# Watching the softmax row sums of a fused attention and feed-forward kernel, with a branch to a general path at its end

## The chip, the core and the metric

The kernel runs on one core of a Trainium2 chip. A core has five engines that work side by side, each with its own in-order instruction queue: TensorE (PE; its weight loads are listed apart as PEld), VectorE (DVE), ScalarE (ACT), GpSimd (POOL) and SyncE (SP, which only issues transfers and waits). DMA engines move data between device memory and the on-chip memory, and also bring in instruction code. The metric is the device time of one execution in microseconds (us); less is better.

## What is computed

```python
k_proj = np.einsum('ks,bhsd->bhkd', E, k)
v_proj = np.einsum('ks,bhsd->bhkd', F, v)
scores = (1 / np.sqrt(64)) * np.matmul(q, k_proj.transpose(0, 1, 3, 2))
scores = scores - np.max(scores, axis=-1, keepdims=True)
attn = np.exp(scores)
attn = attn / (np.sum(attn, axis=-1, keepdims=True) + 1e-09)
attn_out = np.matmul(attn, v_proj)            # (8, 8, 1024, 64)
x = attn_out.transpose(0, 2, 1, 3).reshape(8192, 512)
g, val = x @ w_gate, x @ w_val                # (8192, 1536) each
out = (g * (1 / (1 + np.exp(-g))) * val) @ w_out
```

Keys and values of 8 batches and 8 heads are projected from 1024 rows to 64, attention runs over those 64, and a gated feed-forward layer follows. Inputs and output are float32. q, k and v are normal numbers of size 0.1, so that the scores are small; the kernel before uses that the row maximum cancels and leaves it out: exp of a small score can't overflow.

## The kernel before

**Chunks and tiles.** The 8192 tokens are worked in 16 chunks of 512 (two per batch b, ch = 0 and 1; c = 2b + ch). A chunk's feed-forward has 12 tiles f of 128 hidden columns. For each tile, `f_g` (four matmuls into gps, then tanh on ACT into th) and `f_v` (four matmuls into vps, then two DVE steps, s and hT) run; both use L484 for the matmuls. The output product of a chunk is done one chunk later, in 14 pieces `f_m` of six matmuls (L586), with seven products in place of eight: their operands hs are sums of halves of hT, made on POOL (m = 2 and 5, 128x256 each, L569) and on DVE (m = 1, 6, 7). Small adds on ACT, DVE and POOL (L603 to L621) put the pieces together, and SP stores the rows (L622).

**Attention.** A batch has eight units u, each 128 token rows of four heads. `u_S` makes the scores on PE (L353) and their exp on ACT (ee, L357); `u_R` sums each row of 64 and takes the reciprocal on DVE (zz L368, rr L370, 128x8 each); `u_N` multiplies on POOL (L383) into AA or AAd. For batches 1 to 7 two transposing DMAs on SP turn q (qTd, L330) and the normalised rows (AT, L337) into the layout that PE needs; `u_PVt` then makes the chunk's x (pv, L430). `u_KV` and `u_KT` project keys and values of a batch.

**Order.** Everything stands in an order written out by hand. The main loop runs t = 0 to 191, one feed-forward tile each: `f_g`, slot 2t, `f_v`, the pieces of the chunk before (`late`), slot 2t + 1. Attention steps of batch b are put into slots from 48(b-1) on. In the last batch (b = 7, from slot 288) the last unit's `u_S` is in slot 323, its `u_R` and `u_N` in 324; `u_PVt` follows in slots 332 and 344. An opening before the loop loads E, F, the first k, q, v and the weights piece by piece from POOL's queue (L98 to L136), between them the first four units. POOL issues all loads of the loop as well, in line with its arithmetic. After the loop, `f_m_last` finishes the last chunk: DVE steps (L653) and four stores, two from SP and two from ACT (L669). Then the program closes: SP waits for all transfers and engines, and the engines meet at a barrier (L915).

**Buffers.** PSUM has two banks each for gps, vps and a pool "a" (scores, pv and others), and two for yps. `zz` has three buffers, `rr` four.

Of the kernel before, what the change touches and what calls it, by code (L numbers as in the profile page):

```python
# [9 lines left out]
AF = mybir.ActivationFunctionType  # L10
ALU = mybir.AluOpType
AX = mybir.AxisListType
# [3 lines left out]
B = 8  # L16
# [3 lines left out]
KP = 64  # L20
# [7 lines left out]
CH = 2  # L28
# [10 lines left out]
def kernel(  # L39
# [45 lines left out]
    ET = const.tile([P, NJ, KP], BF16, name="ET")  # L85
    FT = const.tile([P, NJ, KP], BF16, name="FT")
# [8 lines left out]
    def load_k(b, h0=0, h1=H):  # L95
        if b:
            kb[b] = kv_pool.tile([P, H, NJ, D], BF16, name="kb", tag="kb")
        nc.gpsimd.dma_start(  # L98
            out=kb[b][:, h0:h1].rearrange("p h j d -> p h (j d)"),
            in_=k[b, h0:h1].rearrange("h (p j) d -> p h (j d)", j=NJ),  # L100
        )
# [36 lines left out]

    kvp = {}
# [115 lines left out]
    def u_KT(b, at="a", prs=(0, NPAIR)):  # L255
# [5 lines left out]
        for pr in range(*prs) if b > 1 else ():  # L261
# [7 lines left out]
        for g in range(2) if b < 2 else ():  # L269
            turn_ksp(t, b, g)  # L270
# [28 lines left out]
    qT, ee, rr, AA, AT = {}, {}, {}, {}, {}  # L299

# [42 lines left out]
    def u_S(b, u, at="a"):  # L343
# [3 lines left out]
        if (b, ch) in BY_DMA:  # L347
# [3 lines left out]
        for n in range(4):  # L351
            slot = (0, 2, 1, 3)[n] if (b, ch) in BY_DMA else n
# [3 lines left out]
        e = aw.tile([P, 4, 2, KP], FP32, name="ee", tag="ee", bufs=4)  # L356
        nc.scalar.activation(  # L357
# [5 lines left out]
        ee[b, u] = e  # L363

    def u_R(b, u):
        e = ee[b, u]
        z = aw.tile([P, 4, 2], FP32, name="zz", tag="zz", bufs=3)
        nc.vector.reduce_sum(out=z[:], in_=e[:], axis=AX.X)  # L368
        r = aw.tile([P, 4, 2], FP32, name="rr", tag="rr", bufs=4)
        nc.vector.reciprocal(out=r[:], in_=z[:])  # L370
        rr[b, u] = r

    def u_N(b, u, eng=nc.gpsimd):
        ch, w = divmod(u, 4)
        g, i = divmod(w, 2)
        if (b, ch) in BY_DMA:
# [3 lines left out]
        else:  # L380
            a = AA[b, u] = first_batch("a", [P, 2, 4, KP], "AA")
            a = a[:]
        eng.tensor_tensor(  # L383
            out=a.rearrange("p j h k -> p h j k"),
            in0=ee.pop((b, u))[:],
            in1=rr.pop((b, u))[:].unsqueeze(3).to_broadcast([P, 4, 2, KP]),
            op=ALU.mult,
        )

# [324 lines left out]

    with tc.manual_schedule():
# [16 lines left out]
        nc.vector.memset(zeros[:], 0.0)  # L732
        make_identity(nc, ident_fp[:])
# [144 lines left out]

        for t in range(NIT):
# [10 lines left out]
        assert not slots and not late  # L890

# [28 lines left out]
```

## Time and profile before

| | us |
|---|---|
| three runs: median (lowest, highest) | 546.88 (546.44, 546.97) |
| the profiled execution: time, and its span from first to last instruction | 546.79, 545.0 |
| granted TensorE clock | 1.000 |
| u_N on POOL, AAd (L383), one of 128x512 | 1.04 |
| hs sum on POOL (L569), one of 128x256 bf16 | 0.69 |
| row sums and reciprocal on DVE (L368, L370), one | 0.68 and 0.20 |
| median from issue to landing: qb, kb, vb loads | 18.4, 10.6, 15.6 |

The span is what the profiler saw between the first and the last instruction; 1.8 us of the time lie around it. The times of one instruction are means over its group. POOL and DVE are busy for about half and three quarters of the span, and wait for others the rest of it. A clock of 1.000 means that TensorE was never throttled.

### The profile page before, as it was taken

To read this page: it belongs to the slowest core of one execution; us is meant where nothing else is said; L and a number is where in the kernel's file an instruction comes from. 1 tells how busy PE (TensorE), PEld (TensorE's weight loads), DVE (VectorE), ACT (ScalarE), POOL (GpSimd) and SP (SyncE) were. 2 spreads that over 40 slices of the span, in tenths; PEclk is the share of its full clock that TensorE was granted. 3 is DMA by queue.
4 is the path that set the end of the run, shared out by engine and by line. 5 is a ranking of instruction groups with operands and counts; after the bars stand their busy time and mean duration, and the time that the engine had idled before them with its cause. 6 is when DMAs were issued, how large, how long until landed. Compare 5 with 4: busy or idle time off the path is not lost.

```text
span 545.0 us, 9374 instructions
## 1 busy us (share of the span) xinstructions
PE 534.2 (98%) x3494; PEld 313.4 (58%) x3556; DVE 412.8 (76%) x697; ACT 232.8 (43%) x416; POOL 294.2 (54%) x364
## 2 busy tenths in 40 slices
PE   8999999999999999999999999999999999999997
PEld 4654445556556555566565665566655665556565
DVE  3787897779668876789777886787967888676884
ACT  3664453354444434444434444434344433443331
POOL 6952393477616854177631865248660655426162
PEclk9999999999999999999999999999999999999999
DMA  9999989929921599008981199512992133110013
GB/s 202 192 196 191 159 155 187 180 75 160 201 68 40 102 186 215 12 30 146 198 160 38 40 144 209 113 40 55 180 206 64 39 78 79 38 40 12 28 40 118
DMA packets 111631, 62.88 MB, mean 115 GB/s; under 512 B 65888, under 2 KB 102752, under 8 KB 111584
## 3 DMA queue, kind: packets, MB, share of 16 engines
q0 software_dynamic: 43952, 29.49, 38.1%
q1 hardware_dynamic: 66800, 31.20, 27.0%
q10 hardware_dynamic: 832, 1.57, 0.9%
q8 instruction: 28, 0.46, 0.3%
q14 instruction: 19, 0.16, 0.1%
HBM read 60.29 MB, written 16.78 MB: 141 GB/s over the span
## 4 chain that ended last, share of the span: by engine, by line
PE 88%; DMA 8%; POOL 2%; issue 1%; ACT 0%; DVE 0%; POOLq 0%; DVEq 0%; ACTq 0%
PE vps L484 28%; PE gps L484 27%; PE yps L586 25%; DMA qTd<-qb 3%; PE sc L353 3%; DMA qb<-in_q_dram 2%; PE kvp L163 2%; DMA Fraw<-in_F_dram 1%; PE pv L430 1%; PE yps L520 1%; DMA wv<-in_moe_w_val_dram 1%; POOL wv L127 0%; POOL AA L383 0%; POOL wg L127 0%; POOL qb L117 0%
## 5 line engine op out<-in xcount | busy, mean ns | idle before, releaser
L496 ACT ACTIVATE th<-gps 128x512 f32<-128x512 f32 x191 | 114.0, 597 | 198.8 <-PE gps L484 178.1
L484 PE MATMUL vps<-xT,wv 128*128 128x512 bf16 (+1 forms) x754 | 195.3, 377 | 0.9
L484 PE MATMUL gps<-xT,wg 128*128 128x512 bf16 (+1 forms) x734 | 192.4, 377 | 1.4
L503 DVE SCALAR_TENSOR_TENSOR s<-th,gps 128x512 f32<-128x512 f32 x191 | 129.2, 677 | 61.5 <-ACT th L496 60.3
L508 DVE SCALAR_TENSOR_TENSOR hT<-s,vps 128x512 bf16<-128x512 f32 x192 | 132.0, 688 | 21.6 <-PE vps L484 1.5
L569 POOL TENSOR_TENSOR hs<-hT 128x256 bf16<-128x256 bf16 x180 | 120.3, 692 | 49.5 <-DVE hT L508 49.5
L484 PEld LDWEIGHTS <-wv 128*128 128x128 bf16 x776 | 73.1, 98 | 85.0 <-issue 6.7
L586 PEld LDWEIGHTS <-hs 128*128 128x128 bf16 x900 | 88.1, 98 | 34.6 <-issue 0.6
L484 PEld LDWEIGHTS <-wg 128*128 128x128 bf16 x776 | 74.0, 98 | 51.7 <-DMA wg<-in_moe_w_gate_dram 0.3
L616 POOL TENSOR_TENSOR tt<-tt,ysb 128x512 f32<-128x512 f32 x28 | 35.6, 1270 | 109.6 <-DVE tt L615 109.6
L383 POOL TENSOR_TENSOR AAd<-ee,rr 128x512 bf16<-128x512 f32 x56 | 58.4, 1044 | 33.6 <-DVE rr L370 32.3
L586 PE MATMUL yps<-ws,hs 128*128 128x256 bf16 x540 | 68.6, 273 | 0.2 <-DVE ysb L653 0.2
L357 ACT ACTIVATE ee<-sc 128x512 f32<-128x512 f32 x64 | 37.9, 595 | 31.9 <-PE sc L353 30.6
L605 POOL TENSOR_TENSOR tt<-xs 128x256 f32<-128x256 f32 x30 | 29.5, 985 | 38.3 <-ACT xs L603 37.7
L586 PE MATMUL yps<-ws,hT 128*128 128x256 bf16 x360 | 48.8, 273 | 0.3
L586 PE MATMUL yps<-wo,hs 128*128 128x256 bf16 x360 | 48.6, 273 | 0.1
L368 DVE TENSOR_REDUCE zz<-ee 128x8 f32<-128x512 f32 x64 | 43.2, 676 | 5.2 <-ACT ee L357 5.1
L569 DVE TENSOR_TENSOR hs<-hT 128x1536 bf16<-128x1536 bf16 (+1 forms) x49 | 45.2, 928 | 0.1
L586 PEld LDWEIGHTS <-hT 128*128 128x128 bf16 x360 | 35.2, 98 | 16.0
L603 ACT COPY xs<-yps 128x512 f32<-128x512 f32 x30 | 17.6, 585 | 28.0 <-PE yps L586 24.7
L610 ACT COPY ysb<-yps 128x512 f32<-128x512 f32 x30 | 17.6, 585 | 27.5 <-PE yps L586 26.6
L439 ACT CAST xT<-pv 128x512 bf16<-128x512 f32 x56 | 28.7, 600 | 0.0
(100 smaller groups left out, 306.0 us busy)
## 6 DMA issues: line engine op xcount, KB each, us to landing
out_dram<-ysb SPq DMA_DIRECT2D x28, 512.0 KB, 2.7
qb<-in_q_dram POOLq DMA_DIRECT2D x14, 512.0 KB, 18.4
kb<-in_k_dram POOLq DMA_DIRECT2D x7, 1024.0 KB, 10.6
vb<-in_v_dram POOLq DMA_DIRECT2D x7, 1024.0 KB, 15.6
wo<-in_moe_w_out_dram POOLq DMA_DIRECT2D x2, 768.0 KB, 21.8
out_dram<-ysb SPq DMA_DIRECT2D x6, 256.0 KB, 2.4
kraw<-in_k_dram ACTq DMA_DIRECT2D x2, 512.0 KB, 4.8
qb<-in_q_dram POOLq DMA_DIRECT2D x4, 256.0 KB, 7.9
```

The costliest lines, as they stand in the source:

```text
L357: nc.scalar.activation(out=e[:].rearrange("p h j k -> p (h j k)"), in_=ps[:].rearrange("p a k -> p (a k)"), func=AF.Exp, scale=scale,)
L368: nc.vector.reduce_sum(out=z[:], in_=e[:], axis=AX.X)
L383: eng.tensor_tensor(out=a.rearrange("p j h k -> p h j k"), in0=ee.pop((b, u))[:], in1=rr.pop((b, u))[:].unsqueeze(3).to_broadcast([P, 4, 2 ...
L439: nc.scalar.copy(out=xT[b, ch][:, kt, :], in_=ps[:])
L484: nc.tensor.matmul(out=ps[:, ts], lhsT=(wg, wv)[w][:, kt, f * P : (f + 1) * P], rhs=x[:, kt, ts], start=(kt == 0), stop=(kt == NKT - 1),)
L496: nc.scalar.activation(out=th[:], in_=ps[:], func=AF.Tanh, scale=0.5)
L503: nc.vector.scalar_tensor_tensor(out=s1[:], in0=th[:], scalar=1.0, in1=g[:], op0=ALU.add, op1=ALU.mult)
L508: nc.vector.scalar_tensor_tensor(out=hT[c][:, f, :], in0=s1[:], scalar=0.5, in1=ps[:], op0=ALU.mult, op1=ALU.mult)
L569: eng.tensor_tensor(out=hs[c, m][:, fs, :], in0=quarter(hT[c], *a)[:, fs], in1=quarter(hT[c], *b)[:, fs], op=op,)
L586: nc.tensor.matmul(out=ps, lhsT=lhsT, rhs=ws[m][:, f, :] if rhs is None else rhs, start=(start and f == 0), stop=(f == HF - 1), skip_group ...
L605: nc.gpsimd.tensor_tensor(out=t[:, 0], in0=xs[:, 0], in1=xs[:, 1], op=ALU.add)
L616: nc.gpsimd.tensor_tensor(out=t[:], in0=t[:], in1=yo[c, p][:, 1:3], op=ALU.subtract)
```

## The change

It adds up the row sums and their reciprocals of all 64 units in a tile `zsum` on POOL, once per `u_N`. Near the end of the last batch's attention a check reduces `zsum` to one number per partition, compares it with 1e25 (not so for infinities or NaNs), counts the good partitions with one matmul, and writes a flag: 0 if all 128 are good, else 1. Every engine loads the flag into a register. At the end of the program each engine branches on it: if it is not 0, a general path computes the whole output again, with each row's maximum taken out before exp; if it is 0, the program closes. With the inputs given here the flag is 0.

Row sums and reciprocals now share one tile `zr` with four buffers. `maxed` is empty while the ordinary path is laid down, and set in `general`, where it selects other branches of the same Python functions.

```diff
+    zsum = const.tile([P, 16], FP32, name="zsum")
+    sane = const.tile([P, 3], FP32, name="sane")
+    flag = const.tile([1, 1], mybir.dt.int32, name="flag")
...
     def u_R(b, u):
         e = ee[b, u]
-        z = aw.tile([P, 4, 2], FP32, name="zz", tag="zz", bufs=3)
-        nc.vector.reduce_sum(out=z[:], in_=e[:], axis=AX.X)
-        r = aw.tile([P, 4, 2], FP32, name="rr", tag="rr", bufs=4)
-        nc.vector.reciprocal(out=r[:], in_=z[:])
-        rr[b, u] = r
+        zr = aw.tile([P, 2, 8], FP32, name="zr", tag="zr", bufs=4)
+        z, r = (zr[:, i].rearrange("p (h j) -> p h j", j=2) for i in range(2))
+        nc.vector.reduce_sum(out=z, in_=e[:], axis=AX.X)
+        nc.vector.reciprocal(out=r, in_=z)
+        rr[b, u] = (zr, r)
...
     def u_N(b, u, eng=nc.gpsimd):
...
+        zr, r = rr.pop((b, u))
         eng.tensor_tensor(
             out=a.rearrange("p j h k -> p h j k"),
             in0=ee.pop((b, u))[:],
-            in1=rr.pop((b, u))[:].unsqueeze(3).to_broadcast([P, 4, 2, KP]),
+            in1=r.unsqueeze(3).to_broadcast([P, 4, 2, KP]),
             op=ALU.mult,
         )
+        nc.gpsimd.tensor_tensor(out=zsum[:], in0=zsum[:], in1=zr[:].rearrange("p i n -> p (i n)"), op=ALU.add)
...
+    def u_sum():
+        nc.vector.reduce_sum(out=sane[:, 0:1], in_=zsum[:], axis=AX.X)
+        nc.vector.tensor_single_scalar(out=sane[:, 1:2], in_=sane[:, 0:1], scalar=1e25, op=ALU.is_le)
+
+    def u_flag():
+        ps = bank("a", [P, 1], FP32, "bad")
+        nc.tensor.matmul(out=ps[0:1], lhsT=sane[:, 1:2], rhs=sane[:, 2:3], start=True, stop=True)
+        nc.vector.tensor_single_scalar(out=flag[:], in_=ps[0:1], scalar=P - 0.5, op=ALU.is_le)
+
+    def u_bad():
+        bad.append(nc.values_load(flag[:], min_val=0, max_val=1, skip_runtime_bounds_check_because="is_le gives 0 or 1"))
+
+    def general():
+
+        for d in (kb, vb, qb, xT, hT, kvp, qT, ee, rr, AA, AT, hs, xx, zz, tt, yo):
+            d.clear()
+        maxed.append(True)
+        ring["wide"] = False
+        by_dma.extend((0, ch) for ch in range(CH))
+        for b in range(B):
+            load_k(b)
+            load_v(b)
+            u_KV(b)
+            u_KT(b)
+            for ch in range(CH):
+                c = CH * b + ch
+                load_q(b, ch)
+                u_TD(b, ch)
+                for u in range(4 * ch, 4 * ch + 4):
+                    u_S(b, u)
+                    u_R(b, u)
+                    u_N(b, u)
+                u_AD(b, ch)
+                u_PVt(b, ch, (0, 1), ("aa", "yz"))
+                for f in range(NFT):
+                    f_g(c, f)
+                    f_v(c, f)
...
         nc.vector.memset(zeros[:], 0.0)
+        nc.vector.memset(zsum[:], 0.0)
+        nc.vector.memset(sane[:], 1.0)
...
+        for s, fn in ((38, u_sum), (40, u_flag), (46, u_bad)):
+            put(48 * (B - 2) + s, fn)
         for t in range(NIT):
...
         f_m_last(NC - 1)
         assert not slots and not late
+
+    with tc.If(bad[0] != 0):
+        with tc.manual_schedule():
+            general()
```

In slots: `u_sum` is in 326, `u_flag` in 328, `u_bad` in 334. In the built program the five engines' streams up to the branch differ from before by these instructions alone: 64 adds on POOL, two memsets, a reduction and two compares on DVE, one matmul on PE, and a register load on each engine. Behind the branch lie first the general path, then a short block for the flag 0 (each engine raises its semaphore to the value that it would have after the general path; SP does so for eight transfer queues, one after the other), then the closing waits, of which SP now has twelve instead of nine. Instructions of the general path: PE 6,873, ACT 1,158, DVE 1,125, POOL 354, SP 129.

More of the change, by code (lines that the diff above doesn't have):

```diff
@@ L95, in load_k @@
     def load_k(b, h0=0, h1=H):
-        if b:
+        if b or maxed:
             kb[b] = kv_pool.tile([P, H, NJ, D], BF16, name="kb", tag="kb")
@@ L136, in load_wo @@
         )
+    maxed = []
     kvp = {}
@@ L260, in u_KT @@
         t = bank(at, [P, NPAIR, KP], FP32, "kTp")
-        for pr in range(*prs) if b > 1 else ():
+        for pr in range(*prs) if b > 1 or maxed else ():
             nc.tensor.matmul(
@@ L268, in u_KT @@
             )
-        for g in range(2) if b < 2 else ():
+        for g in range(2) if b < 2 and not maxed else ():
             turn_ksp(t, b, g)
@@ L299 @@
     qT, ee, rr, AA, AT = {}, {}, {}, {}, {}
+    by_dma = list(BY_DMA)
     kept = {"q": (0, (5, 2)), "a": (0, (1, 6, 7))}
@@ L346, in u_S @@
         ps = bank(at, [P, 4, P], FP32, "sc")
-        if (b, ch) in BY_DMA:
+        if (b, ch) in by_dma:
             t = qT[b, ch, "d"][:].rearrange("p (h i) t -> p i h t", i=2)[:, i, 4 * g : 4 * g + 4]
@@ L351, in u_S @@
         for n in range(4):
-            slot = (0, 2, 1, 3)[n] if (b, ch) in BY_DMA else n
+            slot = (0, 2, 1, 3)[n] if (b, ch) in by_dma else n
             nc.tensor.matmul(
@@ L356, in u_S @@
         e = aw.tile([P, 4, 2, KP], FP32, name="ee", tag="ee", bufs=4)
+        ee[b, u] = e
+        if maxed:
+            exp_maxed(e, ps)
+            return
         nc.scalar.activation(
@@ L362, in u_S, with exp_maxed @@
         )
-        ee[b, u] = e
+    def exp_maxed(e, ps):
+        m = aw.tile([P, 2, 8], FP32, name="m", tag="zr", bufs=4)
+        s = ps[:].rearrange("p h (j k) -> p (h j) k", j=2)
+        nc.vector.reduce_max(out=m[:, 0], in_=s, axis=AX.X)
+        nc.vector.tensor_scalar_mul(out=m[:, 1], in0=m[:, 0], scalar1=-scale)
+        for i in range(8):
+            nc.scalar.activation(
+                out=e[:, i // 2, i % 2, :], in_=s[:, i], func=AF.Exp, bias=m[:, 1, i : i + 1], scale=scale
+            )
     def u_R(b, u):
         e = ee[b, u]
-        z = aw.tile([P, 4, 2], FP32, name="zz", tag="zz", bufs=3)
-        nc.vector.reduce_sum(out=z[:], in_=e[:], axis=AX.X)
-        r = aw.tile([P, 4, 2], FP32, name="rr", tag="rr", bufs=4)
-        nc.vector.reciprocal(out=r[:], in_=z[:])
-        rr[b, u] = r
+        zr = aw.tile([P, 2, 8], FP32, name="zr", tag="zr", bufs=4)
[3 more added lines that the diff above has]
+        rr[b, u] = (zr, r)
     def u_N(b, u, eng=nc.gpsimd):
@@ L375, in u_N @@
         g, i = divmod(w, 2)
-        if (b, ch) in BY_DMA:
+        if (b, ch) in by_dma:
             if (b, ch, "d") not in AA:
@@ L713, in run_slot @@
             fn(*a)
+    bad = []
+    def u_sum():
[31 more added lines that the diff above has]
+                    f_v(c, f)
+                for m in (1, 2, 5, 6, 7):
+                    h_sum(c, m, 0, HF, nc.vector)
+                for n in range(14):
+                    f_m(c, n)
     with tc.manual_schedule():
```

## The prediction

> **What bounds the kernel now.** I read the page first: busy shares, then the groups, to see which engine has no room.
>
> ```profile
> PE 534.2 (98%) x3494; PEld 313.4 (58%) x3556; DVE 412.8 (76%) x697; ACT 232.8 (43%) x416; POOL 294.2 (54%) x364
> ...
> PE 88%; DMA 8%; POOL 2%; issue 1%; ACT 0%; DVE 0%; POOLq 0%; DVEq 0%; ACTq 0%
> ```
>
> TensorE (PE) is busy 534.2 of 545.0 us and has 88% of the chain that ended last. Anything on PE's own queue costs its own time; work on DVE, ACT or POOL costs nothing until it makes PE wait. The stages show where the remaining idle time lies.
>
> ```profile
> 0.00:60.00 60.00, 56.37 (x393) 30.91 (x398) 41.23 (x80) 30.46 (x61) 32.42 (x46) 1.00 1.32 195
> 60.00:450.00 390.00, 387.33 (x2522) 226.74 (x2572) 304.82 (x512) 169.72 (x300) 220.37 (x267) 1.00 0.69 119
> 450.00:530.00 80.00, 79.53 (x488) 46.77 (x496) 59.48 (x91) 29.69 (x53) 36.19 (x46) 1.00 0.13 40
> 530.00:545.00 15.00, 10.96 (x94) 8.98 (x92) 7.23 (x15) 2.93 (x5) 5.19 (x7) 1.00 0.29 107
> ```
>
> Columns: stage, PE, PE loads, DVE, ACT, POOL busy, clock, DMA. From 60 to 530 us PE is idle 3.1 us of 470. The last 15 us have 4.0 us of idle PE, nearly all of it after its last matmul. So there are three places to price: the opening (PE's waits below), the full middle, and the end.
>
> ```profile
> PE warm L754 <- DVE zeros L732: 1.2, 1, 1.2
> PE sc L353 <- DVE BD L151: 0.7, 1, 0.7
> PE sc L353 <- DMA qTd<-qb: 0.4, 1, 0.4
> ```
>
> The list of PE's waits has no POOL in it at all; the 0.4 us at 59.9 us is the end of a chain of loads that POOL issues. For the end, the records of the output tile and of SyncE (SP):
>
> ```profile
> L669 ACTq DMA_DIRECT2D out_dram<-ysb x2: 363/363/363, 540.1 to 541.7; - x2
> ...
> DMA to landing us min/median/max: 2.0/2.5/3.1
> ...
> SPq L915 <- DMA out_dram<-ysb: 2.3, 3, 1.1
> ```
>
> The last matmul ends at 541.2, the last DVE step at 541.65, ACT's last store is issued 541.68 to 542.04 and lands at 543.82. SP then steps through its closing waits (records 61 ns apart, done at 544.19), and drains and barrier take to 545.03: 1.2 us from landing to end, of which 0.83 after SP's drain. The profiled execution took 546.79 us, 0.09 below the median of 546.88; I add to 546.79.
>
> **The adds (64 on POOL).** Each unit's u_N gets a 128x16 f32 add. No row has that size. POOL's L605 add of 128x256 f32 takes 0.73 us where undisturbed and L616 of 128x512 1.27, so 2.1 ns an element and 0.19 us fixed: 0.22 us. Bounds: 0.10 (POOL's 128x1 memset) and 0.69 (the 128x256 bf16 add, L569). I take 0.22, on the line through the two nearest forms of the same operation. In all 64 x 0.22 = 14 us of POOL, which has 251 us idle. Queued behind an add are the next normalisation, the hs sums, the load issues, and through them the AT transposes on SP. The tightest I find: AT issued at 185.0, landing up to 18.9 us later (203.9), read by pv at 206.3. Cover 2.4 us against 4 x 0.22 = 0.9 in that chunk: price 0 in the middle. Without that cover it would be up to 0.9 a batch, 6 us in all.
>
> In the opening there is less cover. Four adds (three behind normalisations from 13.2 to 18.6 us, one between weight loads) come before the loads that the chain follows to the 59.9 us wait: 0.9 us of later issues. Traffic stands at 195 GB/s over these 60 us, so most of a later issue is absorbed by transfers already queued. Bounds: -0.4 (the wait disappears) and +2.8 (four at 0.69, all passed on); I take +0.2, near the bandwidth-bound case. The two small memsets on DVE lie before a 2.8 us wait for kraw: 0. Sums and reciprocals go to one tile zr instead of two: same operations, still four buffers, now released by the add, under 0.3 us later and four units ahead of reuse: 0.
>
> **The check (slots 326 and 328).** A reduction, two compares on DVE of about 0.20 us each (the 128x8 reciprocal, L370, takes 0.203): 0.6 us, covered by DVE's idle 0.9 us before s in most tiles. The reduction waits for the last add; the last normalisation ends at 458.45, the add about 458.7, and DVE is busy with hT until 458.97: no wait. Then one f32 matmul on PE with one column. The f32 turn of E (L742) does 8 in 1.06 us: 0.13 each. Bounds 0.13 and 0.47 (load and matmul records, 0.20 + 0.27, in series). I take 0.13.
>
> **The register load (slot 334, each engine).** PE's stands between a weight load and its matmul; everything of PE is queued behind it. No row shows such a load. Bounds for its length: 0.05 (PE's event-semaphore records, 51 ns) and 2.14 (the last store's issue to landing, a full trip through memory). But PE's sequencer runs ahead: its semaphore wait before L353 was handled at 104.26, the matmul ran at 105.79, and PE had no gap over 0.05 us there. So 1.5 us is covered, and the price is 0 to 0.64, without that lead up to 2.14. I take 0.1, from the lower half. DVE, ACT, POOL and SP load too; ACT idles 1.78 us before most tanh, and DVE's delay would have to pass two gps banks: 0. [...]
>
> **The branch at the end.** All five streams now jump over the general path: 6,873 instructions on PE, 1,158 on ACT, 1,125 on DVE, 354 on POOL, 129 on SP. Two costs.
> First, more closing steps on SP after the store lands. Before: five waits left, then the drain. After, in the not-taken block: five semaphore steps left after the third store (0.30 us), a branch (about 0.10), then twelve waits (0.73) and the drain (0.07), then 0.83: 543.82 + 2.03 = 545.85, that is +0.82, if every jump is free.
> Second, the jump itself. Instruction code arrives by DMA:
>
> ```profile
> q8 instruction: 28, 0.46, 0.3%
> q14 instruction: 19, 0.16, 0.1%
> ```
>
> Queue 8 fits PE (28 packets of 16 KB are 7,168 instructions of 64 bytes, PE has 7,108); queue 14, with 8 KB packets, then serves the others, 0.1% x 16 x 545 / 19 = 0.46 us each. A target that isn't there must be fetched. Bounds: 0.47 (the packet alone) and 5.2 us (Eraw's read, issue to landing). I take 2.5 (the output's median trip in the quiet end) plus 0.5 = 3.0. SP's stream reaches the branch at 541.4: 544.5; eight steps 0.49, branch 0.1, twelve waits 0.73, drain 0.07, barrier 0.83: 546.7, +1.7. ACT, from 542.05, comes to 545.2 and its semaphore is among SP's last waits: no later. At 5.2 us: +3.9. If SP's short jump finds its code present, ACT decides: 545.25 + 0.9 = 546.15, +1.1.
> [...]
>
> **Sum.** 0.2 + 0.13 + 0.1 + 1.7 = +2.1: 548.9 us.
>
> **The rivals.**
> - The jump hides behind the store's landing (547.7). One mechanism: fetches shorter than 543.82 - 541.4 = 2.4 us on SP and 2.8 us on ACT leave only SP's extra steps, 546.79 + 0.82 + 0.13. For: the packets take under 0.5 us. Against: a trip needs a request and a landing, 2.0 us at the least in any store here. This is not slower, by under 0.2% (1.1 us, about what a measurement of this kernel can tell from no change).
> - PE's register load is not covered. Then up to 2.14 more on PE: 551.0. For: it sits between a weight load and its matmul, and its result has a semaphore of its own. Against: the lead of 1.5 us.
> - The adds break POOL's cover. At 0.69 us four make 2.8, 0.4 over the 2.4 us of cover, in some six batches 2.4, and the opening up to 2.6 more: about 552. Against: PE never waits for POOL now.
> - Faster: later loads at the start leave the transposes alone. All idle of PE before 530 us is 6.8 us; it would have to win 3.2 us to come out 0.2% ahead, at a place where 0.4 is on view.
> - The flag comes out set and the general path runs: over 1,070 us (as many matmuls once more). The sum of positive numbers far below 1e25 is compared, so hardly.
>
> **How the numbers follow.** Forecast 0.58 (its own range 548.1 to 550.8: fetch between 2.4 us and 5), hidden jump 0.16, PE's load 0.13, POOL 0.08, faster 0.02, general path 0.03. Slower 0.58 + 0.13 + 0.08 + 0.03 = 0.82, same 0.16, faster 0.02. The range takes in the hidden jump below and PE's load above: 547.6 to 551.3.
>
> **What would show it.** The span grows by about 2 us; PE's busy time and its 60 to 450 us stage stay within 0.3 us; the last store is issued within 0.6 us of 541.7, and from there to the end it is 5 us instead of 3.35. Wrong: a PE gap near 470 us, PE waits for AT or hs, POOL adds over 0.5 us, or an end that is under 1 us longer.

## The result, and the profile after

| | before | after |
|---|---|---|
| median (lowest, highest), us | 546.92 (546.44, 548.63), 6 runs | 551.56 (550.69, 552.51), 6 runs |
| ratio after / before, 95% interval | | 1.0083 [1.0065, 1.0100] |
| profiled execution: time, span | 546.79, 545.0 | 552.51, 550.6 |
| granted TensorE clock | 1.000 | 0.993 |

The change costs 4.6 us; 2.0 were forecast. The page of the changed kernel, shares and chain:

```profile
PE 535.0 (97%) x3496; PEld 313.7 (57%) x3558; DVE 413.3 (75%) x702; ACT 233.0 (42%) x416; POOL 306.0 (56%) x428
...
q8 instruction: 30, 0.49, 0.4%
q14 instruction: 26, 0.21, 0.1%
...
PE 88%; DMA 8%; ACT 1%; issue 1%; POOL 1%; DVE 1%; DVEq 0%; ACTq 0%
```

PE still sets the time. Its busy time rose by 0.8 us and POOL's by 12, and there are nine more packets of instruction code. The stages (columns: stage, its length, PE, PE loads, DVE, ACT, POOL busy, clock, DMA) show where the 5.6 us of this execution went:

```profile
0.00:60.00 60.00, 55.15 (x385) 30.57 (x390) 40.01 (x80) 30.14 (x60) 34.22 (x54) 0.97 1.27 186
60.00:450.00 390.00, 386.54 (x2517) 225.88 (x2563) 303.63 (x510) 168.61 (x298) 229.10 (x318) 1.00 0.69 120
450.00:530.00 80.00, 79.47 (x486) 46.38 (x495) 60.09 (x95) 30.79 (x54) 35.92 (x49) 1.00 0.14 40
530.00:545.00 15.00, 13.88 (x114) 10.86 (x111) 9.60 (x20) 3.41 (x6) 6.80 (x9) 1.00 0.20 77
545.00:550.60 5.60, 0.00 (x0) 0.00 (x0) 0.00 (x0) 0.00 (x0) 0.00 (x0) 0.65 0.28 95
```

In the first 60 us PE does 1.2 us less work than before, at a clock of 0.97 instead of 1.00. The 0.8 us that PE is less busy from 60 to 450 us is its wait for qTd, which now ends at 62.6 us, inside this stage (at 59.9 before); the rest of the middle is as dense as before. The last 5.6 us hold no computing at all. The finest measure is the step hT, which each of the 192 tiles has once on DVE: its start in this execution against its start before.

| later than before by, us | tile 24 | tile 96 | tile 164 | tile 166 | tile 190 | last DVE step | end of the span |
|---|---|---|---|---|---|---|---|
| after | 2.69 | 2.69 | 2.69 | 2.91 | 2.91 | 2.92 | 5.54 |

Three jumps and nothing else: 2.69 in the opening, 0.22 at the matmul of the check, 2.62 between the last DVE step and the end. From tile 24 to 164 the adds cost nothing, and the register load (between tiles 166 and 168) cost PE nothing. The waits of PE in the opening:

```profile
PE efp L809 <- DMA Eraw<-in_E_dram: 1.5, 1, 1.5
PE warm L821 <- DVE zeros L797: 1.2, 1, 1.2
PE sc L358 <- DMA qTd<-qb: 0.8, 1, 0.8
PE sc L358 <- DVE BD L155: 0.7, 1, 0.7
PE vps L505 <- DMA wv<-in_moe_w_val_dram: 0.3, 1, 0.3
```

Of these, Eraw and wv are new and qTd has doubled. And the end: the last four stores before (line 669), then those after (line 690) and what SP waited for:

```profile
DMA to landing us min/median/max: 2.0/2.1/2.5
```

```profile
L690 SPq DMA_DIRECT2D out_dram<-ysb x2: 344/344/344, 542.6 to 543.9; - x2
L690 ACTq DMA_DIRECT2D out_dram<-ysb x2: 362/366/369, 543.0 to 544.6; - x2
...
DMA to landing us min/median/max: 2.2/4.1/4.4
```

```profile
SPq L961 <- SPq L961: 4.1, 3, 2.9
```

The stores take 4.1 us to land (median) where they took 2.1, and SP stands for 4.1 us at three of its steps behind the branch. How the landings and the steps hang together is taken up with the experiments on the end.

### The profile page after: what moved, and what is told of

The parts are those of the page before. It is cut to its first block, busy times and chain, and to the rows that moved or that the text cites. A ratio compares the mean times of both kernels' runs of the same rounds, so it can differ in the third digit from the quotient of the medians.

```text
span 550.6 us, 9480 instructions
## 1 busy us (share of the span) xinstructions
PE 535.0 (97%) x3496; PEld 313.7 (57%) x3558; DVE 413.3 (75%) x702; ACT 233.0 (42%) x416; POOL 306.0 (56%) x428
## 4 chain that ended last, share of the span: by engine, by line
PE 88%; DMA 8%; ACT 1%; issue 1%; POOL 1%; DVE 1%; DVEq 0%; ACTq 0%
PE vps L505 27%; PE gps L505 27%; PE yps L607 25%; DMA qTd<-qb 3%; PE sc L358 3%; PE kvp L167 3%; DMA qb<-in_q_dram 2%; PE pv L451 1%; PE yps L541 1%; DMA wv<-in_moe_w_val_dram 1%; DMA Eraw<-in_E_dram 1%; POOL wv L130 0%; PE warm L821 0%; ACT ee L366 0%; PE efp L809 0%
## 5 line engine op out<-in xcount | busy, mean ns | idle before, releaser
L403 POOL TENSOR_TENSOR AAd<-ee,zr 128x512 bf16<-128x512 f32 x56 | 58.4, 1044 | 30.9 <-DVE zr L389 30.0
L626 POOL TENSOR_TENSOR tt<-xs 128x256 f32<-128x256 f32 x30 | 28.1, 936 | 36.7 <-ACT xs L624 36.1
L388 DVE TENSOR_REDUCE zr<-ee 128x8 f32<-128x512 f32 x64 | 43.3, 677 | 6.1 <-ACT ee L366 6.0
```

The lines of the kernel that those rows point to most:

```text
L388: nc.vector.reduce_sum(out=z, in_=e[:], axis=AX.X)
L403: eng.tensor_tensor(out=a.rearrange("p j h k -> p h j k"), in0=ee.pop((b, u))[:], in1=r.unsqueeze(3).to_broadcast([P, 4, 2, KP]), op=ALU.mult,
L626: nc.gpsimd.tensor_tensor(out=t[:, 0], in0=xs[:, 0], in1=xs[:, 1], op=ALU.add)
```

## The experiments

Times are medians (lowest to highest). "End" is the time from the end of the last DVE step to the end of the span, 3.38 us before. End, hT and Eraw (its time from issue to landing) are read from one profiled execution of each kernel. The kernels of one group were measured beside the kernel before on the same chip; its medians were 546.70, 546.59, 546.59, 546.69 and 546.76 in the five groups.

### The parts of the change, one at a time

**The adds alone.** No check, register load, branch and general path.

```diff
-        for s, fn in ((38, u_sum), (40, u_flag), (46, u_bad)):
-            put(48 * (B - 2) + s, fn)
...
-    with tc.If(bad[0] != 0):
-        with tc.manual_schedule():
-            general()
```

> The ordinary path with the 64 adds, the shared tile zr and the two memsets; no check, no register load, no branch. Theory A (the opening is later because the first four adds push back the weight and q loads issued on POOL): about 548.1 us, 1.0 to 1.5 over before, all of it gained in the first 60 us of the span, and PE's waits for qTd or weights grow by as much. Rival B (the later opening in the profile of the changed kernel came from the TensorE clock falling to half for 3.4 us, by chance of when its window falls): within 0.4 us of before, and the 60 to 450 us stage the same in both.

Measured: 547.66 (546.97 to 548.62), ratio 1.0019 [1.0010, 1.0028]; end 3.30. The profiled execution took 546.97, the lowest time, and there hT is 0.13 late from tile 24 to the end: nothing in the middle. The 0.96 between the medians is nearest to Theory A, but this execution does not show where it arises; the runs on the opening below do.

**Adds, check and register loads, no branch.**

```diff
-    with tc.If(bad[0] != 0):
-        with tc.manual_schedule():
-            general()
```

> The adds, the check and the register loads, without the branch and without the general path. Theory A (the parts add up, and the short jump of the run with four instructions behind its branch cost nothing): adds run + 0.23 (matmul) + 0.35 (register load on PE) = 547.66 + 0.58 = 548.2, within 0.4 of that run's 547.86; end 3.3 us; markers of hT shift by +0.2 to +0.25 at the matmul (tile 165) and by +0.3 to +0.4 around the load (tile 168). Rival B (matmul and load are covered, and the branch cost the short-jump run its +1.2): within 0.3 of the adds run, 547.4 to 547.9, no shift of the markers. Rival C (the load costs its full trip on PE): over 549.

Measured: 548.09 (547.39 to 548.35), ratio 1.0024 [1.0014, 1.0034]; end 3.33. hT is 1.04 late from tile 24 to 164, 1.26 from 166 to the last step. So the matmul costs 0.22, as in the changed kernel, and the load 0. The 0.35 that the expectation gave to the load came from the last tile (191) read alone; tile 190 before it and the last DVE step behind it show no such shift. Theory A's sum held, with one of its terms wrong; the markers show 0.22 of the 0.5 by which this run's distance to the kernel before exceeds that of the adds alone.

**A branch over four instructions.** Everything but the general path.

```diff
-            general()
+            ysb = yo[NC - 1, 0]
+            nc.vector.tensor_copy(out=ysb[:, 0], in_=ysb[:, 1])
+            nc.scalar.copy(out=ysb[:, 2], in_=ysb[:, 0])
+            nc.gpsimd.tensor_tensor(out=ysb[:, 3], in0=ysb[:, 2], in1=ysb[:, 0], op=ALU.add)
+            nc.sync.dma_start(out=rows_of(NC - 1)[:, 0, 0:HC], in_=ysb[:, 3])
```

> Everything of the change, but the branch's body is one small instruction on each of DVE, ACT, POOL and SP in place of the general path, so that the jump is short (and SP has one semaphore step in the block for flag 0, not eight). Theory A: the end costs 0.4 us over before (SP's longer closing list alone), no engine pauses after its branch, total about 549.1. Rival C (SP's steps): only seven steps of 0.07 us are gone, about 551.0.

Measured: 547.86 (547.80 to 549.27), ratio 1.0024 [1.0013, 1.0035]; end 3.33. A branch over little code costs nothing at the end, not even the 0.4 of Theory A; Rival C falls. Its block for the flag 0 has one semaphore step on SP instead of eight, so that this run says nothing on those eight; a later one does. From here to the changed kernel's 551.56 it is 3.70 us (3.3 to its repeat, 551.14), all from the presence of the general path.

**The branch alone.** No adds, sum and matmul in the ordinary path; the flag is set to 0 at the start, loaded in slot 334, and the branch stands over the whole general path.

```diff
-        nc.gpsimd.tensor_tensor(out=zsum[:], in0=zsum[:], in1=zr[:].rearrange("p i n -> p (i n)"), op=ALU.add)
+        if maxed:
+            nc.gpsimd.tensor_tensor(out=zsum[:], in0=zsum[:], in1=zr[:].rearrange("p i n -> p (i n)"), op=ALU.add)
...
+        nc.vector.memset(flag[:], 0)
...
-        for s, fn in ((38, u_sum), (40, u_flag), (46, u_bad)):
+        for s, fn in ((46, u_bad),):
```

> No adds and no check on the ordinary path; the flag is set to 0 by a memset at the start, each engine loads it in slot 334 and branches at the end over the whole general path. Theory A: the load costs PE 0.35 and the end 2.6 us (code of the jump's target is fetched only when the branch runs), so 549.9 us; the last DVE step to the end of the span takes 6.0 us as in the changed kernel, against 3.4 before. Rival C (the end is longer by SP's additional semaphore steps, the fetch is hidden behind the store's landing): +0.8 at the end, about 548.1 in all.

Measured: 550.47 (549.56 to 552.49), ratio 1.0076 [1.0063, 1.0089]; end 5.66. The branch over the general path alone costs 3.8 us, of which the end shows 2.3, near Theory A; the load's 0.35 in it is not there (hT is 0.29 late from tile 24 to 190).

### The adds in the opening

**Without the first four adds, general path in place.** The row sums of units 0 to 3 of batch 0 are not watched.

```diff
-        nc.gpsimd.tensor_tensor(out=zsum[:], in0=zsum[:], in1=zr[:].rearrange("p i n -> p (i n)"), op=ALU.add)
+        if b or u > 3 or maxed:
+            nc.gpsimd.tensor_tensor(out=zsum[:], in0=zsum[:], in1=zr[:].rearrange("p i n -> p (i n)"), op=ALU.add)
```

> The changed kernel without the adds of the four units in the opening (their row sums are left out of the check). Theory A: about 1.2 us faster than the changed kernel, 550.3, with the opening as before. Rival B: as the changed kernel, 551.5, because the adds had nothing to do with the opening.

Measured: 550.52 (550.17 to 552.27), 1.04 below the changed kernel; end 5.75. The medians speak for the adds, but the profiled execution still had a bad opening, hT 2.56 late. So there are two causes in the opening. The next runs take them apart, first with the branch over four instructions.

**Without the first four adds, short branch.** The same edit on the run with the short branch.

> The run with the short jump (general path left out, four small instructions behind the branch) without the adds of units 0 to 3 of batch 0, whose row sums are not watched. Theory A (those four adds, between the load issues on POOL, cost 0.4 to 1.0 us in the opening): 0.4 to 1.0 us below that run's 547.86, so 546.9 to 547.5 at a time before of 546.6 to 546.7, and the waits for wv and qTd before 62 us are as in the kernel before. Theory B (the four adds cost nothing, the differences of the opening are chance or come from the general path): within 0.3 of 547.86.

Measured: 546.69 (546.45 to 547.01), ratio 1.0001 [0.9992, 1.0010]. Four adds of 64 made 1.17 us of difference, a little more than Theory A's 0.4 to 1.0, and without them the kernel is as fast as before.

**All 64 adds, the first four behind the last load issue, short branch.**

```diff
+        if b or u > 3 or maxed:
+            u_Z(zr)
+        else:
+            held.append(zr)
+
+    held = []
+
+    def u_Z(zr):
         nc.gpsimd.tensor_tensor(out=zsum[:], in0=zsum[:], in1=zr[:].rearrange("p i n -> p (i n)"), op=ALU.add)
...
         load_wo(1)
+        for zr in held:
+            u_Z(zr)
```

> The run with the short jump (general path left out) with all 64 adds, but the adds of units 0 to 3 stand on POOL behind the last weight load (wo) instead of between the load issues. Theory A (what costs is that these adds make the loads behind them late): as the run without them, 546.5 to 547.1, no wait for wv at 21 us and none over 0.4 for qTd at 60 us. Theory B (the adds cost wherever they are, or the buffers held longer make DVE wait): 547.5 to 548.2.

Measured: 546.89 (546.74 to 547.50), ratio 1.0005 [0.9996, 1.0014]. The adds' number costs nothing; their place did. The line of the transposes of q shows the chain, in the run with the short branch and the adds at their first place:

```profile
L335 SPq DMA_TRANSPOSE qTd<-qb x14: 1565/3412/7067, 42.1 to 408.2; - x14
```

and with the four moved:

```profile
L335 SPq DMA_TRANSPOSE qTd<-qb x14: 1568/3534/7170, 40.8 to 405.6; - x14
```

The first transpose starts at 42.1 and 40.8 us (41.15 before). In the trace, the four adds take 0.22, 0.21, 0.66 and 0.25 us on POOL, between 14.2 and 22 us; POOL issues the last three q loads of the opening at 24.84, 25.57 and 30.36 us, and at 23.77, 24.50 and 29.64 with the adds moved (before: 23.73, 24.46, 29.53). The last of them lands at 42.04 instead of 40.80: 0.7 us of later issue became 1.2 of later landing. PE's waits follow, first with the adds in their place, then with them moved:

```profile
PE sc L358 <- DMA qTd<-qb: 0.9, 1, 0.9
PE vps L505 <- DMA wv<-in_moe_w_val_dram: 0.8, 1, 0.8
```

```profile
PE vps L513 <- DMA wv<-in_moe_w_val_dram: 0.9, 1, 0.9
```

The wait for qTd is gone. That for wv at 21 us is not: it comes and goes between kernels (0.3 in the changed one, 0.7 in that with the branch alone, which has no adds), so Theory A had one of its two waits wrong.

**The same order with the general path.** The edit of the last diff, on the changed kernel.

> Whole change, with the adds of units 0 to 3 on POOL behind the last weight load. Theory A: 1.0 to 1.2 us under the changed kernel, 550.2 to 550.7, with the end of 5.7 to 6.0 us unchanged; what then remains over the short-jump run with the same order is the end's 2.6 and whatever the general path's code costs the opening (0 if there is no such cost, 1.0 to 1.4 by the runs so far). Theory B (adds' place is nothing): 551.3 to 552.

Measured: 550.36 (549.58 to 552.09), ratio 1.0068 [1.0056, 1.0080]; end 5.58. This is 1.2 below the changed kernel (0.8 below its repeat in the same group), as Theory A says, and 3.47 above the run with the short branch and the same order: the end has 2.26 more, and some 1.2 remain for the opening.

**The first four adds on DVE, with a prefetch hint.** Directly behind their reciprocals; the hint is that of the next part.

```diff
+        if not b and u < 4 and not maxed:
+            nc.vector.tensor_tensor(out=zsum[:], in0=zsum[:], in1=zr[:].rearrange("p i n -> p (i n)"), op=ALU.add)
```

> As the run with the hint, and the adds of the first four units are done on DVE directly behind their reciprocals, instead of on POOL between the opening's load issues. Theory A (those four POOL adds make later loads late and cost 0.4 to 1.0 us in the opening): 0.4 to 1.0 us below the run with the hint, about 547.3 to 547.9. Rival B (the opening's differences come from when the first loads land and when TensorE's clock steps, by chance): within 0.3 us of the run with the hint, and the waits for Eraw, wv and qTd before 62 us differ no more than they do between runs of the kernel before.

Measured: 551.86 (551.22 to 552.90), 1.0 above the run with the hint alone. Neither theory holds. In its profiled execution PE's clock came up at 10.64 us instead of 6.5, which hides what the adds do; four runs don't settle whether that is their doing.

### The end

**A prefetch hint for the branch.** Although its call is written behind the loop, the hint runs at the start of each engine's stream (0.70 to 0.82 us); the short block lies behind the general path, as in the changed kernel.

```diff
+        tc.mark_branch_hint_location("close", "LikelyTaken", engines=[nc.tensor.engine, nc.vector.engine, nc.scalar.engine, nc.gpsimd.engine, nc.sync.engine])
         f_m_last(NC - 1)
...
-    with tc.If(bad[0] != 0):
+    with tc.If(bad[0] == 0, preferred_fallthrough_block=False, label="close") as arm:
+        pass
+    with arm.Else():
```

> Whole change, but each engine is told at the start of the program, by a branch prefetch hint, that the branch at the end will be taken and where it goes; the general path stays between the branch and its target. Theory A (the end's extra time is the fetch of code that lies behind 6,873 instructions, and the fetch can be made early): the end, from the last DVE step to the end of the span, falls from 6.0 us to 3.3 to 3.9; the last stores land 2.0 to 2.3 us after issue (median) instead of 3.9, because no code packets stand before a sixteenth of theirs; the time is 546.7 + 0.58 (matmul and register load of the check) + 0.4 to 1.4 (opening) = 547.7 to 548.7. Rival B (the hint is lost over 545 us, or the fetch still starts at the branch): end 5.6 to 6.0, time 550.3 to 551.6. Rival C (the far jump is slow for another reason than its fetch, such as a flush of five engines' streams): code packets move to before 541 us, but the end stays above 5 us.

Measured: 550.82 (550.71 to 551.87), ratio 1.0083 [1.0070, 1.0097]; end 6.01. The records of the branches, from the trace (us from the end of the branch's record to the engine's first instruction behind it; for PE the length of its branch record; the last row is the run with the branch over four instructions):

```
                     PE     DVE    ACT    SP
after               4.16   3.54   3.74   2.87
hint                0.48   0.53   1.65   3.06
four instructions   0.23   0.38   0.13   0.14
```

The hint works: PE and DVE no longer stand at the branch, ACT half as long. The end doesn't move, so what PE, DVE and ACT lose at the branch is not what sets it here. Theory A's mechanism is half right, Rival B's numbers are right for another reason. The stores show which:

```profile
L690 SPq DMA_DIRECT2D out_dram<-ysb x2: 344/344/345, 541.0 to 542.3; - x2
L690 ACTq DMA_DIRECT2D out_dram<-ysb x2: 362/368/373, 541.4 to 542.9; - x2
...
DMA to landing us min/median/max: 2.1/3.9/4.4
```

They still land late. The packets in the trace say why. In the changed kernel the third store has 144 packets: 135 run from 544.81 to 545.80, on time, and nine, a sixteenth, from 546.78 to 547.91. Between 544.83 and 547.49 run five packets of code, one of 16 KB and four of 8 KB, nearly one after the other. With the hint it is the same picture, with code between 543.37 and 546.21. In the changed kernel the landings reach SP at 547.25, 548.33 and 548.49, and SP's first steps behind the branch start at 547.27, 548.35 and 548.51: each starts when a store has landed. In the run with four instructions one 8 KB packet comes, after the last store's are through.

ACT's own wait is close behind the stores, though. In the changed kernel ACT is back from its jump at 549.09, and SP asks for ACT's semaphore at 549.61, 0.51 us later; in its repeat and the three other runs of the same layout (the branch alone, without the first four adds, and with these moved) it is 0.13 to 0.38. By this reckoning stores on time alone would have shortened the end by that and no more. In the run with the hint ACT is 2.9 us ahead, and the stores alone hold the end.

**The short block in front of the general path.** The engines run on into it and jump behind it.

```diff
-    with tc.If(bad[0] != 0):
+    with tc.If(bad[0] != 0, preferred_fallthrough_block=False):
```

> Whole change, laid out the other way: the short block for the flag 0 stands directly behind the branch, the general path behind that, so that an engine runs on into the short block and then jumps over the general path to the closing waits. Theory A (any jump over the general path waits for a fetch of code at the end): the short block's steps no longer wait, the jump behind them does; the end is 5.3 to 6.3 us, the time 550.5 to 551.8, and stores still land late by some 1.5 us. Rival B (it is only the place of the short block that costs): end 3.3 to 4.0, time 547.8 to 549.

Measured: 553.27 (552.30 to 554.41), ratio 1.0130 [1.0114, 1.0145]; end 6.81. Theory A's direction, worse than its numbers: PE (4.42), DVE (4.02) and ACT (4.31) wait at the second jump, the stores land up to 4.2 us after issue, and SP goes through the last six of its eight steps behind the last landing before it can jump as well.

**Transfers alone behind the branch.**

```diff
             load_k(b)
             load_v(b)
-            u_KV(b)
-            u_KT(b)
             for ch in range(CH):
-                c = CH * b + ch
                 load_q(b, ch)
                 u_TD(b, ch)
...
+                AA[b, ch, "d"] = aw.tile([P, 4, H, KP], BF16, name="AAd", tag="AAd")
+                nc.vector.memset(AA[b, ch, "d"][:], 0.0)
                 u_AD(b, ch)
...
+                    nc.sync.dma_start(
+                        out=rows_of(CH * b + ch)[:, p::2, :], in_=ysb[:].rearrange("p (j x) d -> p j (x d)", j=2)
+                    )
```

> Whole change, but the general path holds its transfers alone (loads, transposes, stores of all eight batches, 97 instructions on SP and 51 on POOL, one on PE and ACT); its arithmetic is left out. The block for the flag 0 has SP's eight semaphore steps again. Theory A (in the opening the descriptors of the many transfers make the first loads late; at the end SP's eight steps behind the last landing cost 0.8 us by themselves): Eraw takes 5.5 us or more from issue to landing instead of 5.0 to 5.2, the end is 3.3 + 0.8 = 4.1 us with stores landing 2.0 to 2.2 us after issue, time 549.2 to 549.8. Theory B (both come from the size of the code): Eraw 5.0 to 5.2, end as in the run with the short jump, 3.3 to 3.5, time 547.6 to 548.3.

Measured: 549.78 (549.39 to 550.54), ratio 1.0056 [1.0042, 1.0069]; end 5.22; Eraw 5.2. The last landing is at 546.69 and the span ends 2.07 later, where the run with one SP step has 1.26. So SP's eight steps, with the closing waits that they push behind the last landing, cost 0.81, as Theory A and the prediction had it. The last store also landed 3.1 us after issue: its last nine packets start at 545.44, when the first of two 8 KB packets of code (from 545.13 and 545.32) ends. So the end is 1.1 above Theory A's. Eraw was on time, against Theory A: the transfers behind the branch don't delay the opening.

**Code on PE alone**, on the run with the short branch.

```diff
+            t = bank("v", [P, CW], FP32, "far")
+            for _ in range(3436):
+                nc.tensor.matmul(out=t[:, 0:P], lhsT=ident_bf[:], rhs=ident_bf[:], start=True, stop=True)
```

> The run with the short jump, with 3,436 small matmuls (6,873 instructions) added behind PE's branch, so that PE alone has as much code to jump over as in the changed kernel; the general path's other work is left out, and SP has one semaphore step. Theory A (PE's amount of code makes the first loads late in the opening, and PE's fetches hold a part of the last stores): Eraw takes 5.5 us or more, PE's branch takes about 4 us, the last store lands 3 us or more after issue, the end is 4.3 to 5.2 us, time 549.3 to 550.5. Theory B (PE's fetch is over before the last store lands, and the first loads depend on something else): Eraw 5.0 to 5.2, end 3.3 to 3.6 us, time 547.6 to 548.4.

Measured: 551.25 (550.51 to 552.14), ratio 1.0088 [1.0074, 1.0102]; end 4.80; Eraw 5.5. The mechanism is Theory A's: PE's branch takes 3.78, and the stores wait. One 16 KB packet of code runs from 544.23 to 545.28; only then do the held packets of the second store start, and those of the third (546.23 to 546.88) and fourth (546.88 to 547.53) queue behind them:

```profile
L690 ACTq DMA_DIRECT2D out_dram<-ysb x2: 362/366/370, 542.9 to 544.4; - x2
...
DMA to landing us min/median/max: 2.1/3.5/3.8
```

The last landing, at 547.94, is 1.26 before the end. The time is above the expected range since the opening was late as well.

**One batch behind the branch.**

```diff
-        for b in range(B):
+        for b in range(1):
             load_k(b)
             load_v(b)
             u_KV(b)
```

> Whole change, but the general path redoes batch 0 alone (860 instructions on PE, 143 each on ACT and DVE, 46 on POOL, 17 on SP); the other seven batches are left out of it. Theory A (the cost goes with the code jumped over on each engine): SP and POOL jump short, ACT and DVE and PE still fetch, fewer code packets stand before the last stores; the end is 0.8 (SP's eight steps) above 3.3 and up to 1 us more, 4.1 to 5.2 us; Eraw 5.0 to 5.2; time 548.5 to 549.9. Theory B (any taken jump beyond the next packet costs the same): end 5.6 to 6.0 us, time 550.3 to 551.6.

Measured: 550.95 (550.11 to 551.74), ratio 1.0081 [1.0067, 1.0095]; end 5.83; Eraw 5.4. Theory B: a general path of an eighth of the code costs as much at the end. PE's branch over 860 instructions takes 3.98, ACT's over 143 takes 2.77; DVE's over 143 takes 0.52 only. So on PE the distance makes little difference here (4.16 over 6,873 in the changed kernel); why DVE's branch over as many instructions as ACT's takes so much less is not shown.

**Hint and moved adds together.**

> As the run before this one, with the branch prefetch hint on every engine. Theory A (the hint saves the engines' own stall, but code packets still hold a sixteenth of the last stores, and SP's eight steps stay): 0 to 0.8 us under the run before this one, 549.4 to 550.7; end 5.2 to 6.0. Theory B (the hint's better run was chance): same as the run before this one within 0.3.

Measured: 551.01 (549.51 to 552.44), ratio 1.0069 [1.0056, 1.0082]; end 6.32, stores landing up to 4.5 us after issue. Neither theory holds: the hint gains nothing over the moved adds alone (550.36), and the median is 0.65 above them.

### The opening with the general path

**The changed kernel once more**, unaltered.

> The changed kernel unaltered, for a second look at its opening beside the others of this call. Theory A (the general path's code makes Eraw land late): Eraw 5.4 us or more from issue to landing again, wv and qTd waits as in the short-jump run; 551.0 to 552.0. Theory B (the first look was chance): Eraw 5.0 to 5.2, time about 550.5.

Measured: 551.14 (550.48 to 552.78), ratio 1.0084 [1.0071, 1.0097]; Eraw 5.9, end 5.58. Theory A, with hT 2.64 late after the opening.

**Code on DVE, and code on PE**, each on the run with the short branch and the moved adds: 6,872 memsets behind DVE's branch, or the 3,436 matmuls of above behind PE's.

```diff
+            for _ in range(6872):
+                nc.vector.memset(zsum[:], 0.0)
```

> The run with the short jump and the moved adds, with 6,872 small memsets on DVE added behind DVE's branch; the general path's work is left out. Theory A (any engine's amount of code makes Eraw land late): Eraw 5.4 us or more, opening 0.4 to 2.6 us later, DVE's branch takes 2 to 3.8 us; end 3.3 to 4.8 us as code packets hold stores; time 547.9 to 550.5. Theory B (PE's code alone does it): Eraw 5.0 to 5.2, opening as in the run without the memsets, end 3.3 to 4.8; time 546.9 to 548.5.

> The same with 3,436 small matmuls (6,873 instructions) on PE instead of the memsets. Both theories: Eraw 5.4 us or more, an opening 0.4 to 2.6 us later, end 4.5 to 5.0 us as in the earlier run with code on PE alone (4.80); time 548.6 to 550.8. If Eraw lands within 5.2 us, the link between code and opening falls.

Measured, on DVE: 548.09 (547.44 to 548.66), ratio 1.0027 [1.0016, 1.0037]; end 4.22, hT 0.55 early after the opening. On PE: 549.74 (548.94 to 551.27), ratio 1.0054 [1.0042, 1.0067]; end 4.95, hT 2.17 late. The transfers' view (size, median us from issue to landing), DVE first, then PE:

```profile
kraw<-in_k_dram ACTq DMA_DIRECT2D x2, 512.0 KB, 4.7
Eraw<-in_E_dram SPq DMA_DIRECT2D x1, 256.0 KB, 5.2
```

```profile
kraw<-in_k_dram ACTq DMA_DIRECT2D x2, 512.0 KB, 5.2
Eraw<-in_E_dram SPq DMA_DIRECT2D x1, 256.0 KB, 5.7
```

Theory B: it is PE's code. Over all kernels, one profiled execution each: the eight with no or next to no code behind PE's branch have Eraw at 5.0 to 5.2 us, the twelve with 860 instructions or more have it at 5.4 to 6.9. The rows don't say how PE's code does this: kraw's first packets start at 1.9 us in all, and are then slower. That part stays open.

What 0.5 us of Eraw then costs is chance in part, and goes by PE's clock. In the changed kernel, stretches of the opening:

```profile
3.93:7.34 3.41, 1.92 (x12) 1.10 (x11) 0.85 (x2) 0.12 (x1) 3.41 (x6) 1.00 1.22 263
7.34:10.76 3.42, 3.42 (x14) 1.68 (x14) 1.33 (x3) 0.94 (x3) 1.92 (x3) 0.50 1.39 200
10.76:14.17 3.41, 2.48 (x26) 1.68 (x25) 0.93 (x4) 1.88 (x5) 0.74 (x1) 1.00 1.42 200
```

PE's clock had come up at 3.93 us, its 11 warming matmuls ended at 5.1, and PE waited 1.5 us for Eraw. In the next 3.42 us it was busy all the time at half the clock; at the full clock that work would take 1.7 us less (an estimate, half of the 3.42). In the kernel before the clock came up at 6.47 us and stayed up. (The 1.000 given for it counts from there: the warming matmuls ahead of 6.47 us end 0.43 us apart, those behind it 0.21, so PE was not at its full clock from the start.)

Two such first stretches at the full clock, from the run with code on PE alone, where the clock then fell, and from that with the short branch and without the first four adds, where it stayed up:

```profile
4.34:7.75 3.41, 2.28 (x15) 1.40 (x13) 1.28 (x4) 0.63 (x2) 3.41 (x5) 1.00 1.34 249
3.93:7.34 3.41, 2.38 (x15) 1.44 (x13) 1.48 (x3) 0.53 (x2) 3.41 (x6) 1.00 1.30 245
```

This fall of the clock parts the openings of all kernels. In the seven profiled executions that have it, hT at tile 24 is 2.17 to 2.69 late; in the others it lies between 0.55 early and 1.68 late (2.12 in the run with adds on DVE, whose clock came up at 10.64 us). With the first four adds at their place and no fall, runs with code behind PE's branch (1.03, 1.11, 1.68) are as late as those without (0.13, 1.04, 1.10, 1.66). All seven have that code. So what it costs the opening is, by these rows, the fall of the clock; it fell where PE waited 1.1 us or more for Eraw in that stretch, and this wait hangs on the landing of Eraw and on the moment at which the clock came up; no run sets the two apart. The other executions agree in the main: with the general path and the moved adds, the times are 549.58 at a granted clock of 0.999, 549.85 and 550.18 at 0.997, 550.54 at 0.996, 551.99 and 552.09 at 0.995. The changed kernel's six are less orderly (551.26 at 0.999).

## Why the prediction came out as it did

"Slower" was right; the size was not. By medians, in the order in which the parts were put in: all adds with the first four moved, the check, the loads and a short branch +0.2 (546.89 against 546.69); the four adds at their place +1.0 (547.86); the general path +3.7 (551.56), of which 2.2 to 2.7 are the end's and the rest the opening's.

- **Adds in the middle, 0:** right. An add takes 0.22 us (median), as worked out from the two larger forms, and hT doesn't shift from tile 24 to 164. The rival of a broken POOL cover falls for the middle.
- **Adds in the opening, +0.2:** mis-sized; +1.0 to +1.2 by the pairs with the short branch and 0.6 to 1.2 by those with the general path. The chain was the right one (four adds, 0.9 us of later issues: 0.7 to 1.1 measured; one add took 0.66). The step that failed is "most of a later issue is absorbed by transfers already queued": nothing was absorbed, for 0.7 us of later issue of q's last load made its landing, and the first transpose behind it, 1.2 us later than with the adds moved, and PE's wait for it, on view before with 0.4, took that over. The bounds (to +2.8) held it.
- **Check matmul on PE, +0.13:** 0.22, within its bounds. The term counted one step of 0.13; the trace shows this f32 matmul as two records of 0.164, each with a weight load.
- **Register load on PE, +0.1:** 0. The load's record is 0.485 us on PE's queue, under the 1.5 us of lead; the five engines' records are 0.47 to 0.55. The rival that it stays uncovered falls.
- **SP's extra steps, +0.82:** right: 2.07 us from the last landing to the end instead of 1.22; the run with transfers alone shows the same 2.07 without any far jump on PE, DVE and ACT. The 0.10 for a branch in the sum is shown by no run: in the changed kernel SP's first closing wait follows its last step by 0.07 (548.86 to 548.93), and from the last landing (548.49) to that wait it takes 0.44 where the sum has 0.30 + 0.10.
- **The jump, 3.0 us:** too small for the wait (3.5 to 4.2 on PE, DVE and ACT in the changed kernel), though inside its bounds; that the wait is one for code fits the packets of code that run meanwhile (one of 16 KB from 544.83 to 545.78, in PE's 543.01 to 547.17). What failed is the step from it to the end. The sum let SP come late to a store that had landed at its usual time, 2.1 us after issue. In fact, while packets of code run, a sixteenth of the third store waits (nine of its packets, until 546.78), and the last store lands 3.9 us after issue. That is 1.8 us, and with the steps 2.6 instead of 1.7 (2.2 in the repeat). The run with the hint shows it: 0.48 and 0.53 us at the branch on PE and DVE, and the same end. That ACT is "no later" held by 0.51 us only (0.17 in the repeat), since its wait took 3.74. The rival of a hidden jump counted on the same undisturbed landing.
- **Missing altogether:** the general path's code on PE makes the first loads land later (Eraw 5.4 us or more instead of 5.0 to 5.2), and in the seven executions in which PE then waited 1.1 us or more for Eraw its clock fell to half. The sum has no term for either. No view before the change shows the late loads; between pairs of runs that differ in PE's code alone (1.2 and 1.9) or in the whole general path (1.0 and 1.2), 1.0 to 1.9 us are left when the end's share is taken off.
- **Faster, and the general path running:** neither happened.
- **The signs named beforehand:** no PE gap near 470 us, as forecast. PE's busy time and its stage from 60 to 450 us moved by 0.8 where 0.3 was allowed; the stage's 0.8 is the wait for qTd, and hT shows no shift from tile 24 to 164. Four of the 64 adds took 0.66 to 0.96 us, over the 0.5 that was to be a sign against the forecast; the three of them in the middle cost nothing. The last store is issued 2.9 us later instead of within 0.6, which is the opening, and from there to the end it is 6.0 us instead of 5.

The range's upper end, 551.3, was 0.3 below the median. It was built from one rival at a time; the terms that went wrong (adds in the opening, the end, and the opening's cost of code that had no term) add up. That the range came so near owes something to the price of a register load that wasn't there.

## What to carry to other kernels

Work that is put on a queue which issues loads must be priced by the loads behind it, above all in the opening: four adds of 0.2 to 0.7 us cost 1 us there and nothing behind the last issue, with the same instructions. The branch over code that was never run was not free: PE's took 4.16 us instead of 0.23 in the run with four instructions, packets of code ran between 544.83 and 547.49, among the last stores, and those took 4.1 us to land (median) instead of 2.1, so the price is read from the landing of the stores as well as from the branch. The version with moved adds has the lowest median with the whole change in place, 550.36, and none beats the kernel before. When an engine is freed of a wait and the end stays, as with the hint (0.48 us at PE's branch instead of 4.16, the end 6.01 instead of 6.00), the bound was elsewhere: look at what its next step waits for.

## What the runs showed of the hardware

- **While code packets run, a sixteenth of a store waits.** In the changed kernel nine of the third store's 144 packets start at 546.78 or later, while the other 135 are through by 545.80, as if the nine and the code went through one of sixteen transfer engines; in every run with a far jump on any engine the last store lands 2.9 us or more after its issue, against 2.1 before. The code comes on two queues. With code added behind PE's branch alone queue 8 has 30 packets instead of 28, and queue 14 its 19 as before; with code behind DVE's alone queue 14 has 21, and queue 8 its 28. The packets of queue 8 have 16 KB (0.88 to 1.40 us each in the kernel before and the changed one), those of queue 14 have 8 KB (0.31 to 0.89 us). In the kernel before, the 28 and the 19 stand against 7,059 instruction records on PE and 2,315 on the other four engines: 65 and 67 bytes a record, which fits the 64 bytes of the prediction.
- **The clock changed at multiples of 3.41 us.** All times between two changes of the clock are 3.41 us or whole multiples of it (in the changed kernel 3.41, 3.41 and 535.89, which is 157 of them). In seven of the profiled executions the clock came up at 3.9 to 6.3 us and fell to 0.5 one stretch later. In these PE was busy for 1.65 to 2.28 us of the first stretch at full clock and waited 1.1 to 1.7 us for Eraw; where it stayed up, PE was busy for 2.38 us or more, and the longest single wait was 1.0 us.
- **PE's far branches took about the same time.** Over 860 instructions (3.98) or 6,873 (4.16 in the changed kernel), without a hint, PE's branch takes 3.7 to 4.2 us (4.4 at the second jump of the run with the short block in front); over one instruction or none it takes 0.22 to 0.23.
